# W2 and Wo as four lanes of 32-row tiles with turned output, with half of the next chunk's scores inside, and Q, K, V ahead of them

## The chip, the cores and the metric

The kernel runs on one core of a Trainium2 chip. The metric is the device time of one execution in microseconds. The core has five engines with a queue each, worked off in order: TensorE (PE, with its weight loads PEld), VectorE (DVE), ScalarE (ACT), GpSimd (POOL) and SyncE (SP). SP only issues DMAs here; ACT issues some.

## The reference, cut to what matters

S = 2048 tokens, D = 576, 32 heads of 18, a window of 256 keys, F = 4608. The result is a sum of three parts over the same normalised input:

```python
xn = layernorm(x)
q, k, v = split(xn @ wqkv)                       # 32 heads of 18
p = softmax(where(0 <= i - j < 256, q @ k.T * 18**-0.5, -1e9))
a = (p @ v) @ wo
b = (silu(xn @ w1) * (xn @ w3)) @ w2             # 576 -> 4608 -> 576
out = x + a + b
```

## The kernel before, in words

The tokens are cut into four chunks of 512 (`NC`, `CH`). Everything of a chunk is kept in SBUF; weights are streamed anew for each chunk. For each chunk the loop at line 959 writes out the order of the work by hand:

1. **Q, K, V** (`proj_begin`, `proj_part`, line 461; the list `PROJ`, line 486): nine matmul groups in two 64-row lanes. `proj_out` copies the results to `stage` by one DVE and one ACT copy (lines 473, 474) and V straight to `va` (lines 505 to 514). From `stage`, DMAs move the rows of q and k to the partitions on which the scores need them: `span_main` (line 532, issued at 528) and `span_last` (line 544, issued at 559). Two heads share 64 rows; keys lie in blocks of 64, block-diagonal, so that a row of `kv` is cut in runs of 64 keys (128 bytes). The first two q moves go to ACT's queue (`repack_span(0, 1, "act")`), all the rest to SP's.
2. **FFN1** (`unit_pairs`, line 713): 36 units of nine pairs of matmuls, two 64-row lanes of 512 columns, one lane for W1 and one for W3. `unit_tanh` (ACT, line 722) and `unit_h` (DVE, lines 728 and 731) make `hT`. Between the pairs, score steps are spaced by a planner that counts pairs (`spaced_step`, line 1018): `scores` (line 587; a step is 512 columns in both lanes, four heads of one group; eight groups, five steps each, four in chunk 0), `exps` (ACT, line 596), `masks` (POOL, line 623). PV (`pv`, line 644) takes two groups at once in eight small tiles. Its result is turned by DVE (`pv_out`, line 653), scaled (`o_scale`, lines 658, 659), turned back (`o_turn`, line 666) and moved by DMAs into `oT` (`o_pack`, `o_rest`, line 670). PV of groups 0 and 1 stands at unit `FIRST`, of groups 2 to 5 at `JOINT`, of groups 6 and 7 after FFN1.
3. **W2 and Wo** (`p2_list`, `p2_item`, lines 785 and 792): 128 x 128 tiles. The stationary operand is a block of `hT` (128 hidden by 128 tokens), the moving one 288 columns of W2, so that the output has tokens in its partitions. Two halves of D, four banks of PSUM, 36 x 4 matmuls a half, then Wo, then `ofin` = result + x (DVE, line 803) and a store (line 805). The remainder of Wo's rows is `wo_rest` (line 699).

For chunk c the order on TensorE is Q, K, V(c), FFN1(c) with all scores(c), last PV(c), W2 and Wo(c), then Q, K, V(c+1). Only chunk 0's Q, K, V stand ahead of the loop.

Loads: W1 and W3 have three buffers of six parts each (`load_part`, line 322); parts that are due are counted in `owed` and given out one by one behind matmuls (`owe_part`). W2 has four buffers (`NW2`); the first four pieces of a chunk are loaded late in its FFN1, each further one when the last matmul on an old piece has been issued (`load_w2`, line 349; 18 pieces a chunk, 288 KB, in runs of 576 bytes). All of these are on SP's queue, in program order; an instruction there that waits holds all behind it. `xn_send` (line 419) is a DMA transpose of the normalised input into `xnT`, `xn_swap` (line 426) makes the copy with its 64-row halves exchanged, `xnS`.

Synchronisation is by semaphores that `_Prog.resolve` derives from the order of the program and the buffers that each operation names.

Of the kernel before, what the change touches and what calls it, by code (L numbers as in the profile page):

```python
# [164 lines left out]
def bass_parallel_sum__sliding_block__glu_gated_swiglu__prompt_kernel(  # L165
# [32 lines left out]
    with ExitStack() as es:  # L198
# [4 lines left out]
        NXP, NOF, NPT, NW13, NW2, NOD = 7, 4, 10, 3, 4, 2  # L203
        KB, NB, NV = 64, CH // 64, 12
# [12 lines left out]
        wv = sb("wv", [128, 5, D])  # L217
# [8 lines left out]
        kb4 = sb("kb4", [128, G, NV - NB, 2 * KB])  # L226
        va = sb("va", [128, NV, G, 2, VW])
# [35 lines left out]
        th = [sb(f"th{i}", [128, CH]) for i in range(2)]  # L263
# [77 lines left out]

        def load_w2(upto):
            nonlocal n2fill
            if n2fill >= min(upto, NC * 2 * NFC):
                return
            s = n2fill % NW2
            half, fc = divmod(n2fill % (2 * NFC), NFC)
            n2fill += 1
            add("sp", lambda e: e.dma_start(
                w2[s][:], B_w2[fc * 512:(fc + 1) * 512, half * HD:(half + 1) * HD].rearrange("(fl p) d -> p fl d", p=128)),  # L350
                w=[("w2", s)], dma=f"w2_{s}")
# [86 lines left out]
        def proj_part(c, what, banks, part, behind=()):  # L438
# [3 lines left out]
            for n in range(5 - part):  # L442
                for r in range(2):
# [12 lines left out]
                    else:  # L456
                        out_ = PS[:, banks[x], 0:HD]
                        st, mv = xnT[rows, c % 2, kd, i * 128:(i + 1) * 128], wv[rows, kd, x * HD:(x + 1) * HD]
# [9 lines left out]
        def proj_out(c, what, banks, later=None):  # L468
# [11 lines left out]
            else:  # L480
                for r, eng in enumerate(("act", "dve")):
                    move = lambda r=r, eng=eng: v_evac(c, i, b, r, eng)
                    move() if later is None else later[r].append(move)

# [19 lines left out]

        def v_evac(c, tt, b, r, eng):
            pos = (c * NB + 2 * tt + r) % NV
            for p in range(2):
                src = PS[64 * r:64 * r + 64, b:b + 2, 0:HD].rearrange("p b (n e d) -> p e b n d", e=2, d=Dh)[:, p, :, :, :]
                dst = va[64 * p:64 * p + 64, pos, :, :, 0:Dh].rearrange("p (b g) n d -> p b (g n) d", b=2)
                kw = {"j" if p else "w": [("va", pos)]}  # L510
                if eng == "act":
                    add("act", lambda e, dst=dst, src=src: e.activation(dst, src, ACT.Copy), r=[("ps", b), ("ps", b + 1)], **kw)
                else:
                    add("dve", lambda e, dst=dst, src=src: e.tensor_copy(dst, src), r=[("ps", b), ("ps", b + 1)], **kw)
# [29 lines left out]
        def span_last(a, b, only=slice(None)):  # L544
# [3 lines left out]
            for g in order[only]:  # L548
# [6 lines left out]
                for kind, eng, tset, dst, src in moves:  # L555
                    if a == 2:
                        add(eng, lambda e, dst=dst, src=src: e.dma_start(dst, src), r=st_keys(*tset), j=[("k", g)], dma=f"kl_{g}")
                    else:
                        add(eng, lambda e, dst=dst, src=src: e.dma_start(dst, src), r=st_keys(*tset),
                            j=[("k", x) for x in range(a, b)], dma=f"k_{a}")  # L560
# [4 lines left out]

        def keep_keys(g):
            add("pool", lambda e: e.tensor_copy(
                kb4[:, g, :, :].bitcast(dt.float32), kv[:, g, 2 * NB - NV:NB, :].bitcast(dt.float32)),
# [12 lines left out]
        def scores(c, g, s):  # L581
            col = 0
            for n, (kb, q0, nb) in enumerate(steps_of(c)[s]):
                for r in range(2):
# [3 lines left out]
                        out_, kb4[r0:r0 + 64, g, kb + NV - NB, :] if kb < 0 else kv[r0:r0 + 64, g, kb, :], qv[r0:r0 + 64, g, q0 * KB:(q0 + nb) * KB],  # L588
# [37 lines left out]
        def pv(c, j, banks):  # L626
# [4 lines left out]
            for s, st in enumerate(steps_of(c)):  # L631
                col = 0
                for kb, q0, nb in st:
                    n += 1
                    pos = (c * NB + kb) % NV
                    for gi in range(2):
                        g = 2 * j + gi
                        sl = pt_of[(c, g, s)]
                        for pr in range(2):
                            for p in range(2):  # L640
# [5 lines left out]
                                    va[64 * p:64 * p + 64, pos, g, pr, :],  # L646
                                    pt_slot(sl)[64 * p:64 * p + 64, col * KB:(col + nb) * KB, pr],
                                    start=first, stop=(n == n_all), tile_position=(64 * p, 32 * q), skip_group_check=True),
                                    r=pt_keys(sl) + [("va", pos)], **{"j" if any(k[0] == p for k in seen - {(p, gi, pr)}) or not first else "w": [("ps", banks[p])]})
                    col += nb  # L650
# [31 lines left out]
        def o_rest(n, eng):  # L682
# [7 lines left out]
            else:  # L690
                o_move(eng, oT[64:128, 4, CH // 2:CH], oT[0:64, 4, CH // 2:CH], ("oTr", 1), True, "oTr1", [("oTr", 0)])
# [116 lines left out]

        xslot = {}
# [7 lines left out]
        for p in range(2):  # L817
            add("act", lambda e, p=p: e.dma_start(
                wv[64 * p:64 * p + 64, 4, p * HD:(p + 1) * HD], A_wqkv[512:576, 2 * D + p * HD:2 * D + (p + 1) * HD]),
# [22 lines left out]
        vall = va[:, :, :, :, :].rearrange("p t g n c -> p (t g n) c")  # L842
        add("pool", lambda e: e.memset(vall[:, :, Dh:VW], 0.0), w=[("va", i) for i in range(NV)])
        add("pool", lambda e: e.memset(vall[:, :, Dh], 1.0), r=[("va", 0)], w=[("va", i) for i in range(NV)])
# [95 lines left out]
        for what in [("q", 0), ("q", 1), ("q", 2), ("q", 3), ("8", 7), None]:  # L940
            got = proj_begin(0, what) if what else proj_end()
            if got == ("v", 3):
                add("pool", lambda e: e.memset(qv[:, 2:G, :].bitcast(dt.float32), 0.0), r=["wp1", "mk"], w=[("q", g) for g in range(2, G)])
                clear_keys(2, G)
                add("pool", lambda e: e.memset(kb4[:, :, :, :].bitcast(dt.float32), 0.0), w=[("kp", g) for g in range(G)])
# [9 lines left out]
        FIRST = {0: 14, 1: 11, 2: 8, 3: 11}  # L955
        JOINT = {0: (27, 6), 1: (27, 5), 2: (24, 8), 3: (27, 8)}
        AHEAD = [40, 24, 40, 24]

        for c in range(NC):
            NS = len(steps_of(c))  # L960
            att = [(g, s) for g in range(G) for s in range(NS)]
            near = {t: tuple((JOINT[c][0] - 13 + 3 * t if c else 13 + 4 * t) + k for k in (0, 2, 3)) for t in range(3)} | {3: (34, 35, 40)}
            plan = near if c + 1 < NC else {}
            calm = range(9 * JOINT[c][0] + JOINT[c][1] - 8, 9 * JOINT[c][0] + JOINT[c][1]) if c < 3 else ()
            stat, apply, xt = ({v[k]: i for i, v in plan.items()} for k in range(3))
            loads = {8: (2,), 17: (3,)} if c + 1 < NC else {}
            if c == 0:
                loads[4] = (0, 1)
            total = 9 * NF + len(att) + 3 * PV_COST
            if c:  # L970
                total += 9 * sum(COST[kind] for kind, _ in PROJ)
            start = 60 if c == 0 else 42
# [6 lines left out]
            if c:  # L979
                free += [("sh", n) for n in range(4)]  # L980
            held = {6 * NS + 1: free.pop(), 6 * NS: free.pop()}
            early = [("h", n) for n in range(4)] + [("w2", (c * 2 * NFC + n) % NW2) for n in range(NW2)]
            if c:
                early += [("od", n) for n in range(NOD)]
            side = {}
            jobs = {}
            next_pv = 0
# [19 lines left out]
            def score_step():  # L1007
# [7 lines left out]
                if done % (2 * NS) == 0:  # L1015
                    pv_ready[done // (2 * NS) - 1] = clock + PV_AFTER
# [9 lines left out]
            at_u = -1  # L1026
            if c:
                for what in PROJ + [None]:
# [181 lines left out]
```

## Time and profile before

| | |
|---|---|
| time, three runs | 557.65 us median, 557.45 to 557.88 |
| span of the profiled execution, first to last instruction | 555.9 us |
| PE busy | 552.1 us, 99% |
| PEld, DVE, ACT, POOL busy | 346.6, 311.4, 260.0, 162.7 us |
| granted clock of TensorE | 1.000 |
| moved by DMAs | 85.96 MB, 155 GB/s on average |
| packets | 127217, of which 34452 under 512 B |

A profile line names a line of the kernel, an engine and an operation, out<-in by the program's names. A row of the timeline or of the chain begins with its start in microseconds from the span's start and its length; xN is how many instructions are merged. SPq and ACTq are the DMA-issuing instructions of SP and ACT: the time that the engine's queue is taken by them, not that of the transfer. "To landing" is from the issue to the end of the transfer. Matmuls overlap, so the durations of single ones are longer than the steps between them.

### The profile page before, as it was taken

Reading aid. Unit: us, or ns where it says so; the run is one execution under the profiler, and the core shown is the slowest. Engines: PE = TensorE matmul, PEld = TensorE weight load, DVE = VectorE, ACT = ScalarE, POOL = GpSimd, SP = SyncE. Lnnn points to the kernel's source line nnn. Section 1 sums busy time; section 2 is a strip of 40 time slices with the busy share of each in tenths; the row PEclk is TensorE's granted clock in tenths of the full one; section 3 lists DMA queues with packets and bytes.
Section 4 is the critical chain, followed back from the end, with each engine's and each line's share of the span. In section 5 each row is a group of like instructions: output and inputs, shape, how many; then the busy total and the mean of one; then the engine's idle time right before and its main releaser. Section 6 shows DMA issues by size and latency. Waiting matters only on the chain.

```text
span 555.9 us, 15754 instructions
## 1 busy us (share of the span) xinstructions
PE 552.1 (99%) x6772; PEld 346.6 (62%) x6772; DVE 311.4 (56%) x583; ACT 260.0 (47%) x359; POOL 162.7 (29%) x385
## 2 busy tenths in 40 slices
PE   8999999999999999999999999999999999999998
PEld 4666554677665545477766544847776554455776
DVE  6566978610365888851056687874105577678211
ACT  6457766100387774700048787550005777756000
POOL 5424534300034452530003454333001334333000
PEclk9999999999999999999999999999999999999999
DMA  9995989577377469756826748485582674553552
GB/s 244 201 206 139 211 188 243 106 196 186 90 143 164 114 138 167 217 136 174 203 57 140 169 126 198 123 205 136 151 187 54 138 174 122 150 151 82 142 150 65
DMA packets 127217, 85.96 MB, mean 155 GB/s; under 512 B 34452, under 2 KB 124908, under 8 KB 127148
## 3 DMA queue, kind: packets, MB, share of 16 engines
q1 hardware_dynamic: 125523, 83.49, 64.1%
q10 hardware_dynamic: 1624, 1.47, 1.0%
q8 instruction: 53, 0.87, 0.7%
q14 instruction: 17, 0.13, 0.1%
HBM read 71.29 MB, written 2.36 MB: 133 GB/s over the span
## 4 chain that ended last, share of the span: by engine, by line
PE 99%; ACT 0%; DVE 0%; issue 0%
PE ps L713 50%; PE ps L785 25%; PE ps L461 10%; PE ps L587 6%; PE ps L644 3%; PE ps L792 3%; PE ps L827 1%; PE ps L699 0%; PE ps L406 0%; ACT xnT L413 0%; DVE ofin L803 0%; DVE oq L821 0%
## 5 line engine op out<-in xcount | busy, mean ns | idle before, releaser
L713 PE MATMUL ps<-xnT,w 64*128 64x512 bf16 x1400 | 185.4, 376 | 0.0
L713 PE MATMUL ps<-xnS,w 64*128 64x512 bf16 x1120 | 154.0, 376 | 0.0
L785 PE MATMUL ps<-w,hT 128*128 128x288 bf16 x1156 | 146.7, 286 | 0.0
L728 DVE SCALAR_TENSOR_TENSOR gs<-th,ps 128x512 bf16<-128x512 bf16 x144 | 97.8, 679 | 76.6 <-ACT th L722 75.8
L785 PEld LDWEIGHTS ps<-w,hT 128*128 128x128 bf16 x1156 | 112.5, 98 | 28.9 <-issue 0.4
L713 PEld LDWEIGHTS ps<-xnT,w 64*128 64x128 bf16 x1400 | 73.0, 94 | 60.0 <-DVE ofin L653 0.2
L722 ACT ACTIVATE th<-ps 128x512 bf16<-128x512 f32 x144 | 85.6, 594 | 44.4 <-PE ps L713 42.0
L731 DVE SCALAR_TENSOR_TENSOR hT<-gs,ps 128x512 bf16<-128x512 bf16 x144 | 98.9, 687 | 4.9
L713 PEld LDWEIGHTS ps<-xnS,w 64*128 64x128 bf16 x1120 | 58.1, 94 | 46.7
L596 ACT ACTIVATE pt<-ps 128x1024 bf16<-128x1024 f32 (+1 forms) x70 | 70.8, 1011 | 31.2 <-PE ps L587 30.9
L474 ACT ACTIVATE stage<-ps 128x512 bf16<-128x512 f32 x16 | 9.5, 596 | 142.0 <-PE ps L461 142.0
L803 DVE TENSOR_TENSOR ofin<-ps,xp 128x288 bf16<-128x288 f32 x31 | 13.4, 455 | 108.3 <-PE ps L699 58.1
L623 POOL TENSOR_TENSOR hT<-hT,mk 128x128 int32<-128x128 int32 (+1 forms) x59 | 24.0, 429 | 170.5 <-ACT hT L596 170.3
L623 POOL TENSOR_TENSOR pt<-pt,mk 128x128 int32<-128x128 int32 (+1 forms) x124 | 49.9, 427 | 28.8 <-ACT pt L596 28.8
L587 PE MATMUL ps<-qv,kv 64*128 64x320 bf16 (+4 forms) x528 | 52.8, 260 | 0.0
L587 PEld LDWEIGHTS ps<-qv,kv 64*128 64x128 bf16 x528 | 27.4, 94 | 26.2 <-ACT hT L596 1.5
L596 ACT ACTIVATE w<-ps 128x1024 bf16<-128x1024 f32 (+1 forms) x32 | 32.3, 1010 | 12.3 <-PE ps L587 12.2
L461 PE MATMUL ps<-xnT,wp 64*128 64x512 bf16 (+1 forms) x360 | 38.0, 355 | 0.0
L596 ACT ACTIVATE hT<-ps 128x1024 bf16<-128x1024 f32 (+1 forms) x32 | 32.3, 1010 | 5.3 <-PE ps L587 4.8
L623 POOL TENSOR_TENSOR w<-w,mk 128x128 int32<-128x128 int32 (+1 forms) x56 | 22.9, 429 | 28.8 <-ACT w L596 28.8
L666 DVE STREAM_TRANSPOSE od<-oq 128x256 bf16<-128x256 bf16 x64 | 25.8, 427 | 6.9 <-POOL oq L659 6.9
L461 PEld LDWEIGHTS ps<-xnT,wp 64*128 64x128 bf16 x360 | 19.0, 94 | 14.4 <-ACT stage L474 0.2
(93 smaller groups left out, 384.9 us busy)
## 6 DMA issues: line engine op xcount, KB each, us to landing
w<-in_B_w_dram SPq DMA_DIRECT2D x210, 192.0 KB, 3.9
w<-in_B_w_dram SPq DMA_DIRECT2D x72, 288.0 KB, 3.3
xp<-in_A_x_dram SPq DMA_DIRECT2D x30, 144.0 KB, 4.5
out_dram<-ofin SPq DMA_DIRECT2D x31, 72.0 KB, 1.7
xnS<-xnT SPq DMA_DIRECT2D x8, 256.0 KB, 4.2
oT<-od SPq DMA_DIRECT2D x40, 36.0 KB
pt<-in_A_wqkv_dram SPq DMA_DIRECT2D x4, 288.0 KB, 6.0
hT<-in_B_w_dram SPq DMA_DIRECT2D x6, 192.0 KB, 5.2
```

The source lines that it names most:

```text
L461: op = add("pe", lambda e, out_=out_, st=st, mv=mv, n=n, r0=r0, first=first: e.matmul(out_, st, mv, start=first, stop=(part == 1 and n == ...
L587: add("pe", lambda e, r0=r0, out_=out_, kb=kb, q0=q0, nb=nb: e.matmul(out_, kb4[r0:r0 + 64, g, kb + NV - NB, :] if kb < 0 else kv[r0:r0 + ...
L596: add("act", lambda e: e.activation(pt_slot(sl)[:, 0:w, :], PS[:, SC[0]:SC[1] + 1, 0:w].rearrange("p r q -> p q r"), ACT.Exp, scale=scale) ...
L623: add("pool", lambda e, vb=vb, mm=mm: e.tensor_tensor(vb, vb, mm, ALU.mult), r=(key if n == 0 else []) + ["mk"], **{"w" if n == 0 else "j" ...
L644: add("pe", lambda e, p=p, q=q, pr=pr, sl=sl, g=g, pos=pos, q0=q0, nb=nb, col=col, first=first, n=n: e.matmul(PS[32 * q:32 * q + VW, banks ...
L666: add("dve", lambda e: e.transpose(od[i][:, g % 2, c0:c0 + CH // 2], oq[:, c0:c0 + CH // 2]), r=["oq", "oq0"], **{"j" if half or g % 2 els ...
L713: op = add("pe", lambda e, n=n, r0=r0, r=r, k=k, src=src: e.matmul(PS[:, b0 + r, :], wt[r0:r0 + 64, k, fl * 128:(fl + 1) * 128], src, star ...
L722: add("act", lambda e: e.activation(th[i][:], PS[:, bg, :], ACT.Tanh, scale=0.5), r=[("ps", bg)], w=[("th", i)])
L728: add("dve", lambda e: e.scalar_tensor_tensor(out=gs[i][:], in0=th[i][:], scalar=1.0, in1=PS[:, bg, :], op0=ALU.add, op1=ALU.mult), r=[("t ...
L731: add("dve", lambda e: e.scalar_tensor_tensor(out=hT[:, u, :], in0=gs[i][:], scalar=0.5, in1=PS[:, bu, :], op0=ALU.mult, op1=ALU.mult), r= ...
L785: add("pe", lambda e: e.matmul(bank, hT[:, f, tt * 128:(tt + 1) * 128], w2[sl][:, k, n0:n1], start=first, stop=(c + 1 == NC and half == 1 ...
L792: add("pe", lambda e: e.matmul(bank, oT[:, k, tt * 128:(tt + 1) * 128], wo[:, k, d0 + n0:d0 + n1], start=False, stop=(k == 3 and (half == ...
```

## The change

Chunks 0 to 2 are worked in another order; chunk 3's W2 and Wo stay as they were. For c < 3 TensorE now does FFN1(c) with the scores that are left, the last PV(c), Q, K, V(c+1), then W2 and Wo(c) with the scores of chunk c+1's groups 0 to 3 (16 heads) inside, then FFN1(c+1).

- **W2 and Wo** (`w2_lanes`): W2 is now the stationary operand and `hT` the moving one: four lanes of 32 rows, 128 columns of D, 512 tokens. Each lane works its own 32 rows of each block of 128 and has its own bank; the four banks of a group of 128 columns of D are added at its end (`finish`: one ACT copy, three DVE adds), and a DMA transpose on SP turns the result to tokens by D in `fin`. Four such groups; the last 64 columns of D are done by two column tiles of 64 with 256 tokens each. The loop gives the next matmul to the lane that is least far, by a count in rounds of `ROUND`.
- **Scores** of groups 0 to 3 of the next chunk (`scores_new`): one head in one lane of 32 rows, keys in blocks of 128 (`kn`), three steps of 512 columns a head, each of two matmuls in one lane, in the four banks that W2 does not hold; `exps_new` is one bank of 512 columns, `masks_new` on 128-wide blocks. PV of groups 0 to 3 (`pv_new`) has 128 keys in its rows, values in `van`; one of the two calls stands inside the lanes, the other behind them.
- **Q, K, V(c+1)** stand ahead of `w2_lanes(c)`. The moves of groups 0 to 3 are `span_new` (four q and three key moves per call, and one or two of last rows per group); groups 4 to 7 keep `repack_span`. `o_pack(3)` of the last PV goes to SP instead of ACT.
- **W2 pieces** are 9 blocks of 128 rows by 128 columns (runs of 256 bytes), the last two of a chunk 18 blocks by 64 columns (128 bytes); still 18 a chunk, four buffers, SP's queue.
- The sum with x (`fin_add`) and the store (`fin_store`) of chunk c stand in the first units of FFN1(c+1). In FFN1 of chunks 1 to 3 only groups 4 to 7 are scored; PV of groups 4 and 5 stands at unit 20.

```diff
+            if n2fill <= (NC - 1) * 2 * NFC:
+                if m < 16:
+                    dst, f0, nf, d0, nd = w2_by(s, 128), m % 4 * 9, 9, m // 4 * 128, 128
+                else:
+                    dst, f0, nf, d0, nd = w2_by(s, 64), (m - 16) * 18, 18, 512, 64
+                add("sp", lambda e: e.dma_start(
+                    dst, B_w2[f0 * 128:(f0 + nf) * 128, d0:d0 + nd].rearrange("(fl p) d -> p fl d", p=128)),
+                    w=[("w2", s)], dma=f"w2_{s}")
...
+        def span_new(a, b, q_eng="sp"):
+            gs_ = list(range(a, b))
+            moves = []
+            for h in range(4):
+                moves.append(("q", q_eng, gs_, qv[32 * h:32 * h + Dh, a:b, :], stage[Dh * h:Dh * h + Dh, a:b, :]))
+            for h in range(3):
+                r0 = (4 + h) * Dh
+                moves.append(("kn", "sp", gs_, kn[32 * h:32 * h + Dh, a:b, W:W + CH], stage[r0:r0 + Dh, a:b, :]))
+            span_issue(a, b, moves, True)
+            for g in gs_:
+                for dst, src, tset in last_keys(g, slice(W, W + CH), slice(0, CH)):
+                    add("sp", lambda e, dst=dst, src=src: e.dma_start(dst, src), r=st_keys(*tset),
...
+        STEPS = [[(-2, 0, 1), (0, 0, 3)], [(-1, 0, 2), (2, 2, 2)], [(1, 1, 3), (3, 3, 1)]]
+        def scores_new(g, s, a, b):
+            col = 0
+            for n, (jb, q0, nb) in enumerate(STEPS[s]):
+                out_ = PS[:, b, col * 128:(col + nb) * 128]
+                add("pe", lambda e, out_=out_, jb=jb, q0=q0, nb=nb: e.matmul(
+                    out_, kn[32 * a:32 * a + Dh, g, W + 128 * jb:W + 128 * jb + 128], qv[32 * a:32 * a + Dh, g, q0 * 128:(q0 + nb) * 128],
+                    start=True, stop=True, tile_position=(32 * a, 0)),
...
+                if what == "w2":
+                    m = d_ * 4 + k // 9
+                    sl = (c * 2 * NFC + m) % NW2
+                    wt, fl = w2_by(sl, 128), k % 9
+                    add("pe", lambda e, b=b, rows=rows, wt=wt, fl=fl, k=k, a=a, first=first: e.matmul(
+                        PS[:, b, :], wt[rows, fl, :], hT[rows, k, :], start=first, stop=False, tile_position=(32 * a, 0)),
+                        r=[("h", k), ("w2", sl)], **{"w" if first else "j": [("ps", b)]})
+                    if fl == 8:
+                        piece[m] = piece.get(m, 0) + 1
+                        if piece[m] == 4:
+                            load_w2((c + 1) * 2 * NFC)
...
+            if c + 1 < NC:
+                banks = job()
+                pv(c, 3, banks)
...
+                for m, what in enumerate(PROJ + [None]):
+                    got = proj_begin(c + 1, what) if what else proj_end()
...
+                    elif m == 2:
+                        o_turn(7, 0)
+                        o_turn(7, 1)
+                        o_pack(3, "sp")
+                    if got == ("q", 0):
+                        span_new(0, 1, "act")
+                    elif got == ("q", 1):
+                        span_new(1, 3)
+                        owed += 6
+                    elif got and got[0] == "8":
+                        span_new(3, 4)
+                        repack_span(4, G)
+                    owe_part(last_pe())
...
+                late_pv = w2_lanes(c, live, [*JOBS[(i_last - 1) % 3], *JOBS[i_last]])
+                continue
```

426 lines of the change are left out of this document (347 added, 79 removed).

## The prediction

> **What bounds the kernel now.** I read the page's busy shares and its chain first, then the chain in order of time, which says what each stage costs, then the queues of SP and ACT in order of time at the place that the change touches.
>
> ```profile
> PE 552.1 (99%) x6772; PEld 346.6 (62%) x6772; DVE 311.4 (56%) x583; ACT 260.0 (47%) x359; POOL 162.7 (29%) x385
> PE ps L713 50%; PE ps L785 25%; PE ps L461 10%; PE ps L587 6%; PE ps L644 3%; PE ps L792 3%; PE ps L827 1%; PE ps L699 0%; PE ps L406 0%; ACT xnT L413 0%; DVE ofin L803 0%; DVE oq L821 0%
> 101.50:141.90 40.40, 40.40 (x398) 32.08 (x383) 7.58 (x20) 0.21 (x1) 4.92 (x12) 1.00 0.70 169
> ```
>
> TensorE is the chain: 99% of it is matmuls, and nothing else gains unless TensorE's own sum falls. The third row is the W2 stage of chunk 0 (PE, PEld, DVE, ACT, POOL busy, clock, DMA share, GB/s): TensorE full, ACT idle (0.21 us of 40.4), so scores moved there find a free ACT. The stages around the change, in order of time on the chain (start, length, what):
>
> ```profile
> 99.99 1.08 PE ps L713 x10
> 101.07 0.24 PE ps L699 x4
> 101.32 1.01 PE ps L644 x56
> 102.33 16.28 PE ps L785 x132
> ...
> 141.99 9.13 PE ps L461 x100
> 151.12 0.22 PE ps L587 x4
> 151.34 2.51 PE ps L461 x36
> 153.85 0.22 PE ps L587 x4
> ...
> 155.60 0.43 PE ps L713 x4
> ```
>
> One FFN1 pair (two 64-row lanes, 512 columns) takes 1.08/5 = 0.216 us. W2, Wo and the last remainder run from 102.33 to 141.99, 39.66 us. Q, K, V run from 141.99 to 155.60; without the two score steps inside that is 13.17 us. A score step is 0.22 us.
>
> **What the change takes out of TensorE's sum, and what it puts in**, per change of chunk (three of them).
>
> ```profile
> 217.12 2.45 PE ps L644 x176
> 1.24 4.45 PE ps L827 x10
> ```
>
> Before, the parts that it touches: Q, K, V 13.17, W2 and Wo 39.66, first remainder 0.24, twenty score steps (groups 0 to 3, five each) 20 x 0.22 = 4.40, two PVs 2.45 (the first row above is a pair). Together 59.9 us.
>
> After, if nothing waits:
> - four lanes: 4 column groups x 40.5 matmuls of 512 columns a lane. A round of four at the pair's 0.2165 us is 162 x 0.2165 = 35.07. No row here has four row lanes; the pair shows two at full rate, and PV keeps eight small tiles going (96 matmuls in about 1.2 us). So I take full rate; the other end is a rival.
> - 48 score steps, each one round of one lane: 48/4 x 0.2165 = 2.60, against 4.40.
> - a score step is two matmuls in the same lane (128+384, 256+256, 384+128 columns). Matmuls start in order, so the other three lanes sit behind the second one for the length of the first: 53, 107, 160 ns. The gaps between four lanes can hold 217 ns a cycle, so four steps cost 0, 0.21 and 0.42 us beyond that: 0.64 us in 12 steps, 2.6 us in 48. No row has two matmuls running in one lane; the ends are 0 and 48 x 0.107 = 5.1 us. I take the middle.
> - the last 64 columns of D: 41 x 256/512 of 0.2165 = 4.45.
> - PV with 128 keys streams 3072 columns a tile against 2560: 2.45 x 1.2 = 2.94 for two.
> - three more changes of tile shape. The chain has none of them as a gap: 0.1 each (0 to 0.24), 0.3.
>
> With 13.17 for Q, K, V that is 61.1 us, already 1.2 more than before; without the lane blocking it would be 58.5, 1.4 less.
>
> ```profile
> L722 ACT ACTIVATE th<-ps 128x512 bf16<-128x512 f32 x144 | 85.6, 594 | 44.4 <-PE ps L713 42.0
> L623 POOL TENSOR_TENSOR pt<-pt,mk 128x128 int32<-128x128 int32 (+1 forms) x124 | 49.9, 427 | 28.8 <-ACT pt L596 28.8
> ```
>
> On ACT the 48 exponentials have L722's shape, 594 ns: 28.5 us. On POOL 40 masks are 0.43 to twice that: 17 to 34 us. At the end of a column group ACT copies one bank and DVE adds the other three while the lanes go on in the other four banks. All of it lies beside some 43 us of the W2 stage: no cost. If that cover were gone, TensorE would wait a step's 0.6 us each time.
>
> **The step that decides: Q, K, V move ahead of W2, and their moves with them.** Every score needs q and k moved between partitions by DMAs from SP's queue. SP after Q, K, V today:
>
> ```profile
> 145.66 2.59 SPq L528 DMA_DIRECT2D kv<-stage  x3
> 148.30 0.77 SPq L559 DMA_DIRECT2D kv<-stage  x1
> 149.17 1.58 SPq L528 DMA_DIRECT2D qv<-stage  x2
> 150.79 2.47 SPq L528 DMA_DIRECT2D kv<-stage  x3
> 153.31 1.59 SPq L559 DMA_DIRECT2D kv<-stage  x2
> 154.94 4.00 SPq L322 DMA_DIRECT2D w<-in_B_w_dram  x6
> 158.98 1.67 SPq L528 DMA_DIRECT2D qv<-stage  x2
> 160.69 3.49 SPq L528 DMA_DIRECT2D kv<-stage  x3
> 164.23 5.31 SPq L559 DMA_DIRECT2D kv<-stage  x6
> ```
>
> SP issues without a break from 145.66, 3.67 us after Q's start, to 169.54: 28 issues in 23.9 us, and ends 14 us after Q, K, V have ended. It costs nothing today: FFN1 has its weights already. In the changed order W2 follows, and only four of its pieces (the first of four column groups) are loaded ahead. The load of piece 4 is put on SP's queue behind all these moves. How many there are then: group 0 4 (3 keys, 1 last rows; its four q moves go to ACT), o_pack of the last PV 4 (now on SP, not ACT), groups 1 and 2 9, W1/W3 parts 6, group 3 9, groups 4 to 7 9: 41 issues, 13 more.
>
> ```profile
> 282.74 2.59 SPq L528 DMA_DIRECT2D kv<-stage  x3
> 301.67 5.75 SPq L559 DMA_DIRECT2D kv<-stage  x6
> 419.97 2.59 SPq L528 DMA_DIRECT2D kv<-stage  x3
> 439.08 5.41 SPq L559 DMA_DIRECT2D kv<-stage  x6
> 97.86 2.97 SPq L670 DMA_DIRECT2D oT<-od  x4
> L349 SPq DMA_DIRECT2D w<-in_B_w_dram x72: 367/388/1367, 83.9 to 543.7; - x72
> DMA to landing us min/median/max: 2.9/3.3/6.4
> L528 SPq DMA_DIRECT2D qv<-stage x14: 741/795/867, 33.1 to 434.6; - x14
> ```
>
> The same 28 take 23.9, 24.7 and 24.5 us at the three changes (first and last rows above), mean 24.4. Four o_pack add 2.97, nine moves at 1.67/2 add 7.5: 34.9. So SP comes to piece 4 at 3.67 + 34.9 = 38.5 us after Q's start, and it lands 3.3 us later: 41.8. TensorE gets there at 13.17 + 1.4 (ACT's stall, next) + 40.5 x 0.2165 + 14 score steps/4 x 0.2165 = 24.1. It sits idle 17.7 us, in order, with later scores queued behind the waiting matmul. At the shortest issue of this kind (0.741 instead of 0.82) it is 3 us less; at 0.96 (11 in 10.56 us at 158.98 to 169.54) 4 us more; a landing can be 3 us later.
>
> ACT's part, hidden in that idle time: two q moves on ACT hold the second evacuation today.
>
> ```profile
> 145.67 1.53 ACTq L528 DMA_DIRECT2D qv<-stage  x2
> 147.25 0.60 ACT L474 ACTIVATE stage<-ps 128x512 bf16<-128x512 f32 x1 [1.61 <-PE ps L461]
> 147.40 1.28 PE L461 MATMUL ps<-wv,xnT 64*128 64x288 bf16 x18
> ```
>
> The evacuation ends at 147.85, just as the matmuls that reuse its banks start; with four moves it ends 1.5 us later, and TensorE waits about 1.4. It counts only if SP's backlog doesn't.
>
> After the idle time the matmuls are cold. The kernel's first ten full matmuls take 4.45 us (row above), 0.445 each for 512 columns, against 0.2165: 2.3 us lost. The ends are 0 and 2.3; I take 2.3, from the only row after idleness.
>
> **The sum**, from Q's start: 41.8 to piece 4, 2.3 cold, three column groups 121.5 x 0.2165 = 26.3, the other 34 score steps 1.84, lane blocking in them 1.8, PV 2.94, last columns 4.45, tile shapes 0.3: 81.7 against 59.9. 21.8 us x 3 = 65.5. The profiled span is 555.9, so 621.4; the median of the runs, 557.65, lies 1.75 above that span, and with it the time is 623.
>
> **The rivals.**
>
> *Issue time follows the packets: faster.* The key moves become a few 1 KB rows instead of hundreds of 128 B ones, and SP issues a W2 piece of 512 packets in 0.388 us. At that price 41 issues take 16 us, SP reaches piece 4 at 19.6, it lands at 22.9, TensorE needs it at 22.7: no idle time, no stall from ACT either. If the lanes don't block each other, 58.5 against 59.9: 557.65 - 3 x 1.4 = 553.4. It decides at 0.39 us an issue. Against it: q moves of few 1 KB rows cost 0.74 to 0.87 already. 5%. With the blocking it is 561, and prices in between give 561 to 603: 5%.
>
> *W2's pieces starve.* Runs are 256 B (128 columns) instead of 576 B.
>
> ```profile
> DMA packets 1473, 0.18 MB, mean 36 GB/s; under 512 B 1473, under 2 KB 1473, under 8 KB 1473
> q1 hardware_dynamic: 1473, 0.18, 26.1%
> DMA packets 1659, 0.92 MB, mean 184 GB/s; under 512 B 64, under 2 KB 1659, under 8 KB 1659
> q1 hardware_dynamic: 1659, 0.92, 69.7%
> ```
>
> In two 5 us windows (165 to 170, 535 to 540) a 128 B packet holds an engine 0.261 x 80/1473 = 14.2 ns and one of about 555 B 33.6 ns. Between them 256 B is near 20 ns: 1152 packets on 16 engines 1.43 us a piece, where TensorE takes nine rounds, 1.95. At 33.6 ns it is 2.42, and 12 pieces with 9 us of other loads (38 us) outlast the 31 us that use them by 7: 623 + 3 x 7 = 644. 8%. The Trainium skill (DMA: Bandwidth & Descriptors, Specifications) asks for at least 512 B for line rate, which would push towards this end; by the 128 B row the small packet is cheaper, but those stay on the chip, and no run here shows a short read from HBM.
>
> *Four lanes run below four times.* If only as much streams as three lanes hold, a round takes 4/3 x 0.2165 = 0.289 us, and the 130 rounds behind the wait cost 9.4 us more: 623 + 28 = 651. For it: no row has more than two lanes of 512 columns. Against it: the pair loses nothing against one stream, and PV keeps eight tiles going. 7%. The Trainium skill (TensorE: Matmul & The Clock Gate, Measured speedup vs the span model) has 3.07 times for four row tiles of 512 columns, for a single pack; by it a round would be an estimated 0.282 us and the time 649.
>
> **How the numbers follow.** Forecast 75%: 623; its own ends, with SP 3 us shorter, no cold start and no blocking (-7 x 3) or SP and landing later and full blocking (+8 x 3), are 602 and 647. Starved 8% at 644, slow lanes 7% at 651, between 5%, faster 5%. The range that leaves out two in ten is 604 to 648. A difference of 0.2% (1.1 us) is what a measurement can tell from none: faster 0.05, same 0.01 (the edge between the faster rival and the same with blocking), slower 0.94.
>
> **What would show it.** Three idle stretches of TensorE of some 18 us, each about 10 us into W2, ended by the DMA of a W2 piece; SP issuing moves without a break until just before; piece 4's load issued some 24 us after Q, K, V end. Slow matmuls for some 4 us behind each. Lanes: four 32-row matmuls in 0.2165 us. I am wrong if SP is idle when TensorE waits, if the wait is on ACT, or if no wait is over 5 us.

## The result, and the profile after

The changed kernel takes **628.28 us** (median of four runs, 627.15 to 629.75); the kernel before took 557.76 on the same chip (557.45 to 557.88). The ratio is 1.126, with an interval of 1.1245 to 1.1281: slower, 5 us above the forecast of 623 and inside its range. The profiled execution has a span of 625.4 us, 69.5 more than before.

The page after, with the rows that answer to those of before (busy time, TensorE's clock in 40 slices, packets, the chain by engine):

```profile
PE 560.4 (90%) x7690; PEld 311.6 (50%) x7690; DVE 328.3 (52%) x625; ACT 298.7 (48%) x469; POOL 191.8 (31%) x401
...
PEclk9999989985999999999599999999959999999999
...
DMA packets 169218, 88.15 MB, mean 141 GB/s; under 512 B 104260, under 2 KB 166900, under 8 KB 169140
...
PE 82%; SPq 8%; DMA 6%; ACTq 1%; issue 1%; ACT 1%; DVE 1%
```

TensorE's busy time rose by 8 us only, so most of the 69.5 is idle time. TensorE went from 99% of the span to 90%, the chain now leaves it for SP's queue (8%) and for DMAs (6%), and the clock dips to half at three places, one in each change of chunk. The waits of TensorE over the whole span (who waits, for whom, us in total, times, longest):

```profile
PE ps L1011 <- DMA w<-in_B_w_dram: 44.3, 3, 15.5
PE ps L1061 <- DMA w<-in_B_w_dram: 7.2, 6, 1.8
PE ps L842 <- issue: 4.6, 2, 4.4
PE ps L486 <- ACT stage L499: 3.6, 3, 1.2
```

L1011 is the matmul of the four lanes, L1061 that of the last 64 columns of D, L842 FFN1, L486 Q, K, V. Three waits make 44.3 us; all three are for a W2 piece. Now the three changes of chunk, each from the start of Q, K, V to the start of FFN1 (PE, PEld, DVE, ACT, POOL busy, clock, DMA share, GB/s):

```profile
108.66:190.19 81.53, 62.93 (x1087) 38.38 (x1088) 21.76 (x45) 37.85 (x68) 26.52 (x44) 0.90 0.67 131
267.28:347.25 79.97, 62.05 (x1092) 38.71 (x1086) 21.52 (x44) 37.70 (x68) 26.53 (x44) 0.91 0.66 124
424.43:505.76 81.33, 61.51 (x1093) 37.05 (x1086) 21.51 (x44) 37.67 (x68) 26.51 (x44) 0.92 0.63 118
```

They take 242.8 us, against 3 x 59.9 = 179.7 for the same work before: 63.1 us. The other 6.3 us lie in chunk 0: Q, K, V of chunk 1 start at 108.66, and before, W2 started at 102.33. 63.1 + 6.3 = 69.4, which is the whole difference of the spans.

What held the W2 piece is read in SP's queue, in order of time, from the first change (Q, K, V begin at 108.66), with TensorE's row for the end of the wait behind it:

```profile
112.72 2.31 SPq L574 DMA_DIRECT2D kn<-stage  x3
115.07 0.75 SPq L623 DMA_DIRECT2D kn<-stage  x1
115.87 2.94 SPq L799 DMA_DIRECT2D oT<-od  x4
...
138.34 2.47 SPq L574 DMA_DIRECT2D kv<-stage  x3
140.85 3.22 SPq L605 DMA_DIRECT2D kv<-stage  x4
144.12 0.48 SPq L369 DMA_DIRECT2D w<-in_B_w_dram  x1
```

```profile
147.72 0.61 PE L1011 MATMUL ps<-hT,w 32*128 32x512 bf16 x2 [14.53 <-DMA w<-in_B_w_dram]
```

From 112.72 to 144.07 SP issues 41 DMAs with no break; only then comes W2's fifth piece (piece 4), 35.5 us after the start of Q, K, V. It lands 3.6 us later. TensorE had been at that matmul since 133.19.

### The profile page after: what moved, and what is told of

The parts are those of the page before. It is cut to its first block, busy times and chain, and to the rows that moved or that the text cites. A ratio compares the mean times of both kernels' runs of the same rounds, so it can differ in the third digit from the quotient of the medians.

```text
span 625.4 us, 17823 instructions
## 1 busy us (share of the span) xinstructions
PE 560.4 (90%) x7690; PEld 311.6 (50%) x7690; DVE 328.3 (52%) x625; ACT 298.7 (48%) x469; POOL 191.8 (31%) x401
## 4 chain that ended last, share of the span: by engine, by line
PE 82%; SPq 8%; DMA 6%; ACTq 1%; issue 1%; ACT 1%; DVE 1%
PE ps L842 45%; PE ps L1011 14%; PE ps L486 6%; PE ps L914 6%; DMA w<-in_B_w_dram 5%; SPq L574 4%; PE ps L666 3%; PE ps L723 2%; SPq L605 1%; PE ps L773 1%; ACTq L574 1%; DMA pt<-in_A_wqkv_dram 1%; PE ps L738 1%; PE ps L1020 1%; PE ps L1061 1%
## 5 line engine op out<-in xcount | busy, mean ns | idle before, releaser
L842 PE MATMUL ps<-xnT,w 64*128 64x512 bf16 x1400 | 178.9, 377 | 4.6 <-issue 4.6
L1011 PE MATMUL ps<-hT,w 32*128 32x512 bf16 x1728 | 113.6, 391 | 44.3 <-DMA w<-in_B_w_dram 44.3
L842 PE MATMUL ps<-xnS,w 64*128 64x512 bf16 x1120 | 149.2, 377 | 0.0
L857 DVE SCALAR_TENSOR_TENSOR gs<-thb,ps 128x512 bf16<-128x512 bf16 x144 | 98.0, 680 | 70.8 <-ACT thb L851 70.3
L851 ACT ACTIVATE thb<-ps 128x512 bf16<-128x512 f32 x144 | 85.6, 595 | 59.3 <-PE ps L842 58.3
L842 PEld LDWEIGHTS ps<-xnT,w 64*128 64x128 bf16 x1400 | 67.8, 94 | 76.4 <-issue 6.3
L1011 PEld LDWEIGHTS ps<-hT,w 32*128 32x128 bf16 x1728 | 60.9, 96 | 77.4 <-DMA w<-in_B_w_dram 47.3
L753 POOL TENSOR_TENSOR pt<-pt,kv 128x256 int32<-128x256 int32 x96 | 58.1, 628 | 106.1 <-ACT pt L746 105.3
L842 PEld LDWEIGHTS ps<-xnS,w 64*128 64x128 bf16 x1120 | 54.5, 94 | 57.0 <-issue 0.4
L746 ACT ACTIVATE pt<-ps 128x512 bf16<-128x512 f32 x120 | 74.4, 784 | 12.8 <-PE ps L738 12.8
L675 ACT ACTIVATE pt<-ps 128x1024 bf16<-128x1024 f32 (+1 forms) x46 | 46.2, 1005 | 47.3 <-PE ps L666 47.3
L738 PE MATMUL ps<-qv,kn 18*128 18x384 bf16 (+2 forms) x288 | 55.1, 273 | 0.0
L675 ACT ACTIVATE hT<-ps 128x1024 bf16<-128x1024 f32 (+1 forms) x20 | 20.0, 1002 | 42.1 <-PE ps L666 42.0
L486 PE MATMUL ps<-xnT,wp 64*128 64x512 bf16 (+1 forms) x360 | 39.1, 355 | 0.2 <-DVE va L538 0.2
L914 PE MATMUL ps<-w,hT 128*128 128x288 bf16 (+1 forms) x292 | 36.9, 284 | 0.0
L738 PEld LDWEIGHTS ps<-qv,kn 18*128 18x128 bf16 x288 | 27.0, 96 | 14.0 <-issue 0.7
```

Of the source, the lines that this page charges most:

```text
L486: op = add("pe", lambda e, out_=out_, st=st, mv=mv, n=n, r0=r0, first=first: e.matmul(out_, st, mv, start=first, stop=(part == 1 and n == ...
L675: add("act", lambda e: e.activation(pt_slot(sl)[:, 0:w, :], PS[:, SC[0]:SC[1] + 1, 0:w].rearrange("p r q -> p q r"), ACT.Exp, scale=scale) ...
L738: add("pe", lambda e, out_=out_, jb=jb, q0=q0, nb=nb: e.matmul(out_, kn[32 * a:32 * a + Dh, g, W + 128 * jb:W + 128 * jb + 128], qv[32 * a ...
L746: add("act", lambda e: e.activation(pt_slot(sl)[:, :, p], PS[:, b, :], ACT.Exp, scale=scale), r=[("ps", b)], **{"j" if p else "w": pt_keys ...
L753: add("pool", lambda e, b0=b0, nb=nb, k0=k0: e.tensor_tensor(v[:, b0:b0 + nb, :], v[:, b0:b0 + nb, :], mkn[:, k0:k0 + nb, :], ALU.mult), r ...
L842: op = add("pe", lambda e, n=n, r0=r0, r=r, k=k, src=src: e.matmul(PS[:, b0 + r, :], wt[r0:r0 + 64, k, fl * 128:(fl + 1) * 128], src, star ...
```

## The experiments

My theory: SP's queue of moves holds piece 4, and this is most of the loss. The rivals at this point: the pieces' short runs (256 and 128 bytes) keep the DMA engines from delivering; the four lanes, or two matmuls in one lane, run slower than counted. For each kernel the table has the start of chunk 1's Q, K, V and the length of the three changes, in us, read off TensorE's rows in order of time; the time is the median of the runs.

| kernel | Q, K, V(1) at | change 1 | change 2 | change 3 | time | ratio to before |
|---|---|---|---|---|---|---|
| before (the same work) | 102.3 | 59.9 | 59.9 | 59.9 | 557.7 | 1 |
| the change | 108.6 | 81.5 | 80.0 | 81.3 | 628.3 | 1.1245 to 1.1281 |
| nine moves left out | 109.5 | 73.1 | 73.6 | 73.4 | 607.0 | 1.0855 to 1.0916 |
| runs of 576 bytes | 109.1 | 77.6 | 78.2 | 80.3 | 621.0 | 1.1114 to 1.1159 |
| one matmul a score step | 109.3 | 82.4 | 84.3 | 82.0 | 632.2 | 1.1304 to 1.1369 |
| moves merged and spread | 108.7 | 70.0 | 66.2 | 65.0 | 586.3 | 1.0503 to 1.0562 |
| the same, 576 bytes | 109.2 | 64.6 | 62.4 | 61.5 | 575.4 | 1.0284 to 1.0348 |
| only the first keys' moves later | 103.0 | 88.6 | 80.8 | 81.4 | 628.5 | 1.1244 to 1.1306 |
| merged and rebalanced | 102.5 | 78.3 | 62.8 | 64.2 | 585.9 | 1.0479 to 1.0519 |
| the same, first keys by ACT | 102.5 | 71.1 | 64.0 | 62.7 | 576.4 | 1.0305 to 1.0402 |
| the same, 576 bytes | 103.7 | 69.4 | 63.5 | 63.9 | 575.9 | 1.0281 to 1.0335 |

**1. Nine moves left out.** It leaves the moves of groups 4 to 7 out at the three changes, so those groups are scored with old keys and queries.

```diff
                     elif got and got[0] == "8":
                         span_new(3, 4)
-                        repack_span(4, G)
```

> Leaves out the moves of q and k of groups 4 to 7 at the three changes of chunk (9 of the 41 issues that stand ahead of W2's piece 4 on SP); those groups are then scored with chunk 0's q and k. SP-backlog theory: piece 4 is issued 9 x 0.79 = 7.1 us earlier, TensorE's wait falls from 14.8 to 7.7 us, 628.3 - 21 = 607 us. Rival (the wait is the transfer of the 256-byte runs, or its congestion): the wait stays, 628 within 2 us.

Measured 607.0 us. TensorE's waits, and the first of them in order of time:

```profile
PE ps L1011 <- DMA w<-in_B_w_dram: 22.6, 4, 8.0
```

```profile
141.23 0.60 PE L1011 MATMUL ps<-hT,w 32*128 32x512 bf16 x2 [7.00 <-DMA w<-in_B_w_dram]
```

The wait at piece 4 shrinks from 14.5 to 7.0 us at the first change, by the 7 us that nine issues take (9 x 0.77). Piece 4 itself, its runs and its buffers are as before: what held it was its place in the queue. The bytes of the nine moves have gone too, but they can't have held it for long: in the changed kernel it landed 3.6 us after its issue, against 3.3 for a piece before.

**2. Runs of 576 bytes.** W2's pieces are read as in the kernel before (four blocks of 128 rows by 288 columns, the same bytes); the lanes read them as if they were in the new order, so W2's part of the result is that of reordered weights, at the same amount of work.

```diff
             n2fill += 1
-            if n2fill <= (NC - 1) * 2 * NFC:
...
-                return
             add("sp", lambda e: e.dma_start(
                 w2[s][:], B_w2[fc * 512:(fc + 1) * 512, half * HD:(half + 1) * HD].rearrange("(fl p) d -> p fl d", p=128)),
```

> All W2 pieces loaded with 576-byte runs as in the kernel before, same bytes, same number of loads; the weights then lie wrongly, so the result differs. SP-backlog theory: the wait at piece 4 stays between 13 and 15 us; only the waits at the last columns (7.2 us in all) go: 628.3 - 8 = 620. Rival (short runs cause the wait): the wait at piece 4 falls below 5 us and the time below 600.

Measured 621.0 us. TensorE's waits (L1002 are the lanes and L1052 the last columns here):

```profile
PE ps L1002 <- DMA w<-in_B_w_dram: 44.9, 3, 16.2
...
PE ps L1052 <- DMA w<-in_B_w_dram: 0.7, 2, 0.3
```

The three long waits stay (44.9 us for 44.3), and the waits at the last columns, where the pieces had runs of 128 bytes, go from 7.2 to 0.7 us. Short runs cost 7 us in the changed kernel; they are not the long waits.

**3. One matmul a score step.** Each new score step is one matmul of 512 columns instead of two in the same lane, against one block of keys, so the scores of groups 0 to 3 are those of other keys.

```diff
-            for n, (jb, q0, nb) in enumerate(STEPS[s]):
+            for n, (jb, q0, nb) in enumerate([(s, 0, 4)]):
```

> Each new score step is one matmul of 512 columns in its lane instead of two of the same total; the scores of groups 0 to 3 are then of other keys. Theory that a second matmul in one lane doesn't hold the other lanes: the same within 1.5 us. Theory of the prediction (lane blocking, 1.8 us a chunk behind the wait): 628.3 - 5.4 = 623.

Measured 632.2 us. If a second matmul in a lane held the others up, the lanes would run faster here. The stretch of the first change between the PV and the next DMA wait holds the third and fourth group of columns but for the third's first 16 W2 matmuls: 272 of them in both kernels, and 23 score steps. In the chain of the changed kernel and then of this one (start, length, what):

```profile
163.15 0.98 PE ps L1011 x12
...
180.68 5.27 DMA w<-in_B_w_dram
```

```profile
164.29 0.32 PE ps L1011
...
181.80 5.74 DMA w<-in_B_w_dram
```

17.53 and 17.51 us: nothing is gained. The time met neither expectation: it is 3.9 us above the change, where at most 1.5 or a gain of 5.4 was expected. The lanes don't explain that, but waits and the clock do. At change 2, 4.3 us longer than in the changed kernel, the wait at piece 4 is 15.6 us (14.3 there), the half clock behind it lasts some 5.8 us (4.5), and a wait of 2.75 us at the last columns up to 345.41 is followed by a second half clock, until 349:

```profile
347.00:348.00 1.00, 1.00 (x14) 0.86 (x12) 0.00 (x0) 0.00 (x0) 0.00 (x0) 0.50 0.97 267
```

In the changed kernel the same place has two waits of 1.0 us, and the clock is 1.00 behind them. Why the waits themselves are longer here is open.

**4. Moves merged and spread.** One call moves groups 1 to 3 instead of two; the last eleven moves are given out one by one between the W2 loads; six W1 and W3 parts go out late in FFN1 instead of in Q, K, V, and the copy `xnS` is made later in the lanes (round 60 instead of 12).

```diff
-                    elif got == ("q", 1):
-                        span_new(1, 3)
-                        owed += 6
+                    elif got == ("q", 2):
+                        span_new(1, 4)
                     elif got and got[0] == "8":
-                        span_new(3, 4)
-                        repack_span(4, G)
+                        hold = moves_ = []
+                        spread_last()
+                        repack_span(4, G)
+                        hold = None
...
+        W2_EVENTS = {n: ("move",) for n in (10, 13, 16, 19, 22, 25, 28, 31, 34, 37, 39)} | {60: ("swap",), 70: ("xs",), 76: ("xs",), 82: ("xs",), 88: ("xs",), 94: (0,), 98: (1,),
```

> Nothing left out: the moves of groups 1 to 3 merged into one set (11 issues instead of 18), the last 11 moves given to SP one by one between W2's loads 4 to 7, six W1/W3 parts per chunk loaded in the last units of FFN1 instead of in Q, K, V. SP-backlog theory: the three waits of 14.8 us at piece 4 vanish and with them some 3 us each of half clock: 628.3 - 3 x 17.7 = 575 us, granted clock 1.00; what is left over 558 is the wait for ACT in Q, K, V (1.2 each), for the 128-byte pieces (2.4 each) and 4.4 us in chunk 0. Rival (transfer of 256-byte runs): over 5 us of wait per chunk remain and the time stays over 590.

Measured 586.3 us: 42 us less than the change, but 11 more than I expected. TensorE's waits, and the DMA packets of the second change's W2 stage:

```profile
PE ps L1026 <- DMA w<-in_B_w_dram: 9.4, 10, 1.9
PE ps L1076 <- DMA w<-in_B_w_dram: 5.4, 6, 1.2
```

```profile
DMA packets 23600, 7.70 MB, mean 168 GB/s; under 512 B 21431, under 2 KB 23375, under 8 KB 23593
```

No wait for W2 is over 2 us any more, and the mean clock is back at 0.994. What is left at W2 is sixteen small waits, 14.8 us in all, and in that stage nine packets in ten are under 512 bytes and the DMA engines are busy for a share of 0.91:

```profile
269.20:315.00 45.80, 42.38 (x825) 23.41 (x821) 12.12 (x24) 33.92 (x58) 25.21 (x42) 1.00 0.91 168
```

That points to the rival of the starving pieces, which was no bound while SP held them; kernel 5 tests it.

**5. The same with runs of 576 bytes**, with W2's part that of reordered weights as in 2.

> The merged kernel (586.3 us) with W2's pieces in 576-byte runs, same bytes; the weights then lie wrongly. Theory that, with SP's backlog gone, the transfer of the short runs is the second bound (waits for W2 pieces 14.8 us in all, DMA engines full from 145 us on): those waits fall below 4 us, and the time by 8 to 15 us, to 571 to 578. Rival (what is left is SP's queue still): the waits stay and the time is within 3 us of 586.

Measured 575.4 us, as the theory of the short runs has it; the waits for W2 fell from 14.8 to 5.0 us, not quite below the 4 expected. The waits, and the third change:

```profile
PE ps L1017 <- DMA w<-in_B_w_dram: 4.7, 7, 0.9
...
PE ps L477 <- ACT stage L490: 3.6, 3, 1.2
```

```profile
390.71:452.17 61.46, 59.38 (x1086) 36.91 (x1088) 21.47 (x45) 37.61 (x68) 26.57 (x44) 1.00 0.65 147
```

This third change, 61.5 us of which TensorE waits 1.2 for ACT and 0.9 for a DMA, is nearly free of waits. TensorE's own work is 59.4 us in it (the PE column), and 60.4 and 59.9 in this kernel's other two changes: 59.9 on average, as long as before. The order itself has hardly anything to win.

**6. Only the first keys' moves later.** Chunk 0 has eight moves more (`first_prev`, the last keys of chunk 0 for chunk 1's scores), which stand at unit 20 of FFN1, ahead of W1 and W3's parts. Here they stand at unit 34.

```diff
                     add("dve", lambda e: e.memset(wz[:], 0.0), w=["wz"])
+                if c == 0 and u == 34:
                     first_prev()
```

> The changed kernel with the eight moves of chunk 0's last keys given to SP at unit 34 instead of unit 20, nothing else. If the 4.4 us that TensorE waits near 85 us are the W1/W3 parts queued behind these moves, that wait goes and the time falls by 4 to 6 us, to 622 to 624. If not, 628.

Measured 628.5 us: no gain, and my expectation failed. Chunk 0's FFN1 ends 5.6 us sooner (Q, K, V(1) start at 103.0), but the first change takes 7.1 us more. SP's row of the eight moves, in the changed kernel:

```profile
75.59 6.42 SPq L637 DMA_DIRECT2D kn<-stage  x8
```

The same in this kernel:

```profile
105.92 6.30 SPq L637 DMA_DIRECT2D kn<-stage  x8
```

Then this kernel's DVE in order of time, where it waits for them, and its TensorE:

```profile
113.46 0.69 DVE L498 CAST stage<-ps 128x512 bf16<-128x512 f32 x1 [8.03 <-DMA kn<-stage]
```

```profile
114.21 2.31 PE L486 MATMUL ps<-xnT,wp 64*128 64x512 bf16 x10 [6.49 <-DVE stage L498]
...
150.18 0.61 PE L1011 MATMUL ps<-hT,w 32*128 32x512 bf16 x2 [13.02 <-DMA w<-in_B_w_dram]
```

SP comes to the moves at 105.92 only, when Q, K, V(1) have begun. They read `stage`; DVE has to wait with the next chunk's K until they have, and TensorE with it. The cost of the eight issues has changed its place, not gone.

**7. Merged and rebalanced.** Kernel 4 with these eight moves at unit 34, W1 and W3's parts at the start of Q, K, V, the loads of x in FFN1's first units, and two of group 0's four q moves on SP.

```diff
-                moves.append(("q", q_eng, gs_, qv[32 * h:32 * h + Dh, a:b, :], stage[Dh * h:Dh * h + Dh, a:b, :]))
+                moves.append(("q", q_eng if h < 2 else "sp", gs_, qv[32 * h:32 * h + Dh, a:b, :], stage[Dh * h:Dh * h + Dh, a:b, :]))
...
+                load_w13((), 6)
                 for m, what in enumerate(PROJ + [None]):
...
+                later(0, lambda c=c: fin_xs.extend([load_x((c - 1) * TB + k) for k in range(TB)]))
```

> The merged kernel with every other load taken out of the W2 stage (six W1/W3 parts at the start of Q, K, V, where SP is idle; the loads of x into FFN1's first units), two of group 0's four q moves on SP instead of ACT, and the moves of chunk 0's last keys at unit 34 instead of 20. By the terms of the prediction without waits and without lane blocking a change of chunk takes 58.5 us against 59.9: 557.7 - 4 = 554; with half a microsecond of wait at a few places 554 to 560. If short runs starve W2 even alone, over 565.

Measured 585.9 us, 26 to 32 more than I expected. The largest single part is the same as in 6, 11 us in TensorE's row of chunk 1's Q, K, V:

```profile
118.27 2.31 PE L486 MATMUL ps<-xnT,wp 64*128 64x512 bf16 x10 [11.05 <-DVE stage L498]
```

The waits at W2's pieces are another 11.3 us, where I had expected half a microsecond at a few places, and behind the long wait the clock is at half here too, until about 122.6.

**8. The same, first keys by ACT.** The eight moves are issued by ACT, one in every second unit from 20. Against kernel 7:

```diff
-            for n, (dst, src, tset) in enumerate(moves):
-                add("sp", lambda e, dst=dst, src=src: e.dma_start(dst, src), r=st_keys(*tset), dma="knp",
...
+            return [lambda n=n, dst=dst, src=src, tset=tset: add("act", lambda e: e.dma_start(dst, src), r=st_keys(*tset), dma="knp",
...
-                if c == 0 and u == 34:
-                    first_prev()
+                if c == 0 and 20 <= u < 36 and u % 2 == 0:
+                    if u == 20:
+                        prevs = first_prev()
+                    prevs.pop(0)()
```

> The rebalanced kernel, with chunk 0's eight moves of the scores' earlier keys issued one by one by ACT in every second unit of FFN1 from unit 20, so that they stand neither ahead of W1 and W3's parts on SP nor late enough for the next K to wait for the staging tile. In the rebalanced kernel TensorE waited once for that tile, 11.1 us, in chunk 0's Q, K, V. If that wait was all that hid the rebalancing's gain, the time falls by it from 585.9 to about 575 us. If the moves only hand the wait on to W2's first pieces, it stays within 583 to 587.

Measured 576.4 us, 9.5 less than 7: the wait for the staging tile has gone and the time with it, though the 554 to 560 expected of 7 are still far. TensorE's waits, and the window of the second change's W2 stage:

```profile
PE ps L1025 <- DMA w<-in_B_w_dram: 11.5, 11, 2.5
PE ps L751 <- DMA qv<-stage: 3.0, 1, 3.0
```

```profile
264.10:308.00 43.90, 39.53 (x785) 21.68 (x789) 10.20 (x20) 32.55 (x54) 24.79 (x42) 1.00 0.79 136
```

The waits at the last columns and for ACT, which kernel 4 still had, are not in the list; what is left is at W2's pieces, some of which still stand between moves on SP, and at a q move.

**9. The same with runs of 576 bytes**, with W2's part that of reordered weights as in 2.

> The same with W2's pieces read in runs of 576 bytes, as in the two kernels before with such runs; the numbers that come out use W2's entries in another order. The short runs were worth 11.0 us to the merged kernel (586.3 to 575.4), so about 564 us if the two add up: still above the kernel before (557.8), since the lanes' own work in a change is no shorter than that of the old order. If the two do not add up, 570 to 575; under 557 the account of the lanes' own work is wrong.

Measured 575.9 us, the same as 8 by the intervals: the two remedies do not add up. One reason may be that kernel 8 had already taken the loads of x out of the W2 stage: the DMA share there is 0.79, against 0.91 in kernel 4. Still, the waits at W2's pieces fall from 11.5 to 8.3 us here:

```profile
PE ps L1016 <- DMA w<-in_B_w_dram: 8.3, 6, 2.5
```

Much of that gain goes to the clock. The second change in kernel 8, then here (PE busy is the second number, the clock the third from the end):

```profile
250.81:314.84 64.03, 59.66 (x1087) 35.70 (x1088) 21.45 (x45) 38.12 (x68) 26.52 (x44) 1.00 0.76 135
```

```profile
250.24:313.75 63.51, 60.97 (x1089) 36.54 (x1084) 21.49 (x44) 38.10 (x68) 26.57 (x44) 0.97 0.62 133
```

TensorE is busy for 1.3 us more with the same work. Its only wait for W2 in this change is one of 2.15 us, up to 277.31, and behind it the clock is at half from about 278.4 to 281.9; the third change is alike, with one wait of 2.55 us. In kernel 8 the second change has three waits for W2, of 0.8, 0.6 and 2.5 us, and the clock stays at 1.00.

The table shows one more thing about 7 to 9. Chunk 0 ends 5 to 6 us sooner in them than in the changed kernel, but the first change takes 6 to 16 us longer than the second: much of the relief comes back there as waits and half clock.

No version that I ran beats the kernel before. The best third change (61.5 us) is still over the 59.9 of the old order. With no waits at all the order would by the PE columns of kernel 5 gain an estimated 3 x 0.5 = 1.5 us at best (59.4), and nothing by their mean (59.9); no run here is free of waits.

## Why the prediction was right, point by point

**SP's backlog: right, and shown.** The 41 issues took 31.4 us, not 34.9 (0.77 us each instead of 0.85), and SP came to piece 4 at 35.5 instead of 38.5. TensorE got there at 133.19, 24.5 after the start (24.1 predicted). The idle time was 14.8 us on average, not 17.7. Taking nine issues away took (44.3 - 22.6)/3 = 7.2 us off each wait (kernel 1), spreading the issues took the long waits away (kernel 4). The 0.85 came from SP's rows of before; the new key moves, in long rows, take 0.73 to 0.82 in their three rows, 0.77 on average (2.31/3 at 112.72), the old ones 0.82 (2.47/3 at 138.34). The rival in which the issue time falls to a W2 piece's 0.39 is refuted: longer rows saved some 0.05 us an issue, if anything. None of the three signs of an error came: SP was not idle, the long waits were not on ACT, and none was short.

**ACT's moves: right.** 1.4 predicted, 1.2 measured in each change (L486 on ACT's `stage`). I counted it inside the idle time, and it is hidden there.

**The cold clock: right.** 2.3 predicted. The windows of the changed kernel, first the stretch ahead of the first wait, then those behind it, and the ones in which the clock comes back behind the other two:

```profile
123.57:133.04 9.47, 9.47 (x187) 5.10 (x187) 0.86 (x3) 8.79 (x16) 5.50 (x9) 1.00 0.66 145
...
152.00:153.00 1.00, 1.00 (x17) 0.52 (x13) 0.00 (x0) 0.38 (x1) 0.91 (x2) 0.50 1.34 217
153.00:154.00 1.00, 1.00 (x22) 0.54 (x14) 0.00 (x0) 0.58 (x2) 0.00 (x0) 0.76 0.84 138
...
310.00:311.00 1.00, 1.00 (x21) 0.48 (x17) 0.00 (x0) 0.23 (x2) 0.87 (x2) 0.76 1.34 218
...
467.00:468.00 1.00, 1.00 (x21) 0.33 (x16) 0.74 (x2) 0.42 (x1) 0.00 (x0) 0.75 1.33 217
```

TensorE restarts at 147.72 with a clock of 0.50 and is at full rate from about 153.5: 5.8 us at half rate, so 2.9 us lost. At the other two changes it restarts at 306.03 and 464.30 and has its clock back in the middle of the windows shown, after some 4.5 and 3.2 us: 2.2 and 1.6 lost, 2.2 on average.

**The lanes: full rate, right; the blocking, wrong.** The first row above is one group of columns with 13 score steps: (40.5 + 13/4) x 0.2165 = 9.47 us. The window is cut to that length and TensorE is busy in all of it; the group's last matmul ends at 133.19, 0.15 us later, and a single matmul lasts 0.16 us longer than a step (0.38 against 0.22). So four lanes of 512 columns run at the pair's rate. The Trainium skill (TensorE: Matmul & The Clock Gate, Measured speedup vs the span model) has 3.07 times for such a pack; no slowing of that kind is in this trace, where a long stream has a round of four each 0.2165 us. And the two matmuls of a score step do not hold the other lanes: I had put 1.8 us behind the wait for that, and the lanes of kernel 3 are no faster without it. The rival at 651 us is refuted.

**Starving pieces: no bound for the changed kernel, but the next one.** At 217 GB/s (row 152.00:153.00) a piece of 288 KB takes 1.36 us; I had worked out 1.43. The middle pieces never starve. What I missed are the last two pieces of a chunk, with runs of 128 bytes: 7.2 us of waits at L1061 in all, 2.4 a change. Kernel 2 takes them away. Kernels 4 and 5 show the rest: with SP's backlog gone, the short runs cost 11 us. With runs of 576 bytes the engines moved 303 GB/s (kernel 2, 150.4 to 151), against the 217. The Trainium skill's 512 bytes for line rate (DMA: Bandwidth & Descriptors, Specifications) pointed at a true cost, in the wrong place for this forecast.

**What I missed: chunk 0.** The change also adds eight moves to SP in chunk 0's FFN1, and I counted the moves of the three changes only. SP was behind there, and W1 and W3's parts came late. The chain of the changed kernel:

```profile
84.14 3.92 DMA w<-in_B_w_dram
88.05 1.23 issue
89.28 2.32 PE ps L842 x10
```

That is the 4.4 us wait of L842; the half clock behind it, 0.50 from 89.28 until about 92, costs 1.4 more, and the two make 5.8 of chunk 0's 6.3 us. The prediction counted every issue that stands ahead of piece 4 and none that the change adds elsewhere; each instruction that is added counts in its queue too.

**The sum came out closer than its terms, by luck.** Per change 81.7 was predicted, and 81.5, 80.0 and 81.3 measured. At the first change SP 3.0 earlier and no blocking (1.8) stand against a landing 0.3 later, the waits at the last columns (2.5 there), the longer half clock (0.6), and 1.3 us in smaller pieces, of which two can be named: 0.4 for PV's wait for DVE, and 0.4 for the last columns' own matmuls, 4.9 us instead of 4.45. Some 4.8 us too much and 4.7 too little cancel. The 5 us by which the time is above the forecast are chunk 0's 6.3, less 65.4 - 63.1 = 2.3 in the three changes, and 1.1 by which the median lies above the profiled execution's own time.

## What to carry to other kernels

A queue that ends long after its stage is harmless only while the next stage has its data; before work is moved ahead, count every issue that then stands between the new consumer and its load (here 41 x 0.77 us against 24.5 us). When a wait is taken away, look for the next bound of the same stage: here SP's queue, then short runs, then the tile that the late moves still read. And first ask what the new order is worth without any wait: here 59.4 to 60.4 us against 59.9 a change, a prize of 0.5 us at best for which a 14 us wait was risked.

## What the runs showed of the hardware

The half clock's length varies: after 14 to 16 us of idleness TensorE ran at half rate for 5.8, some 4.5 and some 3.2 us at the three changes. The Trainium skill (TensorE: Matmul & The Clock Gate, Part 1: The HAM clock gate) has about 3.4 us and says that it varies from run to run; here it varies within one execution. Nor does it take a long idle time: in kernel 9 a wait of 2.15 us is followed by some 3.4 us at half clock (278.4 to 281.9), while in kernel 8 one of 2.53 us, up to 284.32, is not (the clock is 1.00 from 284 to 290). What decides between them is open.

The new exponentials were dearer than their shape says. Three groups of the changed kernel, the second with every second 2-byte element of `pt` as its output:

```profile
L851 ACT ACTIVATE thb<-ps 128x512 bf16<-128x512 f32 x144 | 85.6, 595 | 59.3 <-PE ps L842 58.3
...
L746 ACT ACTIVATE pt<-ps 128x512 bf16<-128x512 f32 x120 | 74.4, 784 | 12.8 <-PE ps L738 12.8
...
L675 ACT ACTIVATE pt<-ps 128x1024 bf16<-128x1024 f32 x38 | 38.9, 1024 | 36.1 <-PE ps L666 36.0
```

The first (tanh) and the second (exp) have 512 columns from PSUM, and the second takes 784 ns against 595. I had costed it at 594; it stayed hidden beside the W2 stage. The function is not the cause: the old exponentials (L675), which write `pt` without gaps, take 1024 ns for 1024 columns and 916 for 896, so an estimated 592 for 512. That leaves the layout of the output as the likely cause; no run tries it apart.
